# Two strips in one output tile, some stores issued by ScalarE, and a new order of work, in an attention and gated-convolution kernel

## The chip, the core and the metric

The kernel runs on one core of a Trainium2 chip. The metric is the device time of one execution in microseconds (us), as the median of several executions. The core's engines work side by side: TensorE does matmuls (PE; its weight loads are PEld), VectorE (DVE), ScalarE (ACT) and GpSimd (POOL) do elementwise work, and SyncE (SP) issues DMAs. ScalarE can issue DMAs as well; these are listed under ACTq, those of SyncE under SPq.

## What is computed

The reference is two stages of attention with 32 learned points, and a gated convolution behind it (B=4, N=12800, C=128, 32 inducing points, 5 taps):

```python
def mab(q, kv):
    s = scale * (q @ kv.transpose(0, 2, 1))
    a = np.exp(s - s.max(-1, keepdims=True))
    a /= a.sum(-1, keepdims=True) + 1e-09
    return a @ kv
h = mab(I, x)          # 32 rows per batch, a sum over all of x
y = mab(x, h)          # 12800 rows per batch, 32 weights each
...
for k in range(K):
    gate_pre += conv_w[k][None, None, :] * yp[:, k:k + S, :]
gate = 1.0 / (1.0 + np.exp(-gate_pre))
out = (gate * (y @ w_val)) @ w_out
```

Since y is 32 weights per row times h, the kernel never writes y: five taps and the value product are six small matrices of 32x128 per batch (W), which are applied to the 32 softmax weights of each row (P).

## The kernel before, in words

**Tiles.** A batch of 12800 rows is cut into four strips of 3200, which lie side by side: a strip takes 32 of the 128 partitions or columns of PE. The strips are cut into chunks of 128 to 512 columns (SIZES), 29 chunks in all over the four batches. An array `seqs` numbers them from 0 to 28; the last one, 28, has 160 columns, number 27 has 512.

**Stages of a batch**, each an item of the list ORDER (lines 957 to 998) by a short name:

- `l`, `k`: loads of x by SP, `xt` with channels on partitions (load_xt, L359) and `xk` with rows on partitions (load_xk, L370). For batch 0 nearly all of xk is made by transposes on PE instead (`x`, make_xk, L397) and evicted by ACT (L402) or DVE (L404), as XEV says.
- `s1` (L422): scores of a chunk against the 32 points, evicted by DVE with the maximum (L430). `gm` (gmax, L441 to 457): the maximum of a group of chunks (GROUPS), over the strips on POOL.
- `h` (L465 to 497): exponentials on ACT, a transpose on DVE, and the matmuls of xk that sum h (L486).
- `u`, `t`, `w`, `W`, `po`: preparation: h from the groups' sums (u, L528 to 536), its transpose (t, L545), the small matrices in two fp16 parts (w, L565 to 603; the last inputs are written in L587 and L603), their transposes onto the strips (W, L621, evicted in L629 and L631), and the scaled output weights (po).
- `s2` (L691 to 749): scores of a chunk against h, softmax over 32 on DVE, POOL and ACT, into P in two fp16 parts.
- `r` (rblock, L763 and L772): a row block. It runs gate and value matmuls of up to three neighbouring chunks on the four row groups of PE at the same time. Two row blocks belong to a chunk. `begun` (L188) splits the gate units (15 per strip) over neighbouring blocks; the constant EVEN weighs an even split. Behind it come tanh on ACT (L833), the product of gate and value on DVE (L843), and two fp16 parts of it (halves: L856 on ACT, L861 on POOL, tile `gl`).
- `o` (outp, L865): the output matmul of one strip of a chunk (three fp16 matmuls, L881 to L883; for chunk 28 one fp32 matmul, L874), its eviction with scaling by DVE or ACT (L891 or L893; DVE where 4 x chunk + strip stands in OUTV), and its store by SP (L898). The tiles are `os`, four buffers; in the last two chunks `et`, `pt` and `ss`, which are free by then.
- `z` (idle, L917): n matmuls on zeros, which compute nothing that is used.

**What sets the order.** PE follows ORDER as it stands. Everything else is ordered by a planner in the kernel itself (Plan.order and Plan.lay, L79 to L184): it lays the operations on their engines with the durations in COST, the DMA rate BW, and due times worked out backwards from PE's list, and takes at each moment the ready operation with the earliest due time, less the operation's entry in URGE. SP issues in the order that results. A load planned when AHEAD or more row blocks are already in the list waits for the row block that many back (`ago`, L332). BUFS gives the buffers of each tile: 11 for xt, 4 for xk, 4 for os, 4 PSUM banks `a`.

The output function before, cut to the choice of tiles and the store:

```python
        if k >= len(seqs) - 2:
            os = ("ss" if k == len(seqs) - 1 else ("et", "et", "et", "pt")[r], "out", b, c, r)
        ...
        def store():
            nc.sync.dma_start(out[b, :, r, FIRST[b][c]:FIRST[b][c] + n], st[os][:, :n])

        op("SP", n * 512 / BW, store, [j], 0.0, [], [os])
```

Of the kernel before, what the change touches and what calls it, by code (L numbers as in the profile page):

```python
# [20 lines left out]
P = 128  # L21
# [28 lines left out]
class Plan:  # L50
# [85 lines left out]
    def lay(self, deps, succ, topo, nominal):  # L136
# [18 lines left out]
        while len(seq) < n:  # L155
# [14 lines left out]
            if e == "SP":  # L170
                bus = max(bus, start) + ops[i]["dur"]
                end[i] = max(bus, start + 0.5) + (1.7 if start < 10.0 else 2.6)
                free[e] = start + 0.4
# [39 lines left out]
def tile_kernel(ctx: ExitStack, tc: tile.TileContext, xt, xk, indT_in, w64, out):  # L213
# [651 lines left out]
    def outp(k, r):  # L865
# [4 lines left out]
        if k >= len(seqs) - 2:  # L870
            os = ("ss" if k == len(seqs) - 1 else ("et", "et", "et", "pt")[r], "out", b, c, r)
        if k == len(seqs) - 1:
# [14 lines left out]

        def ev():
            o, a = sb(pw, os, [P, 512])[:, :n], st[key][:, :n]
            if v:  # L890
                V.tensor_scalar(o, a, st["osc", b], None, ALU.mult)  # L891
            else:
                S.activation(o, a, AF.Copy, scale=st["osc", b])  # L893

        j = op("DVE" if v else "ACT", cost("psum", n) + 0.07 if v else cost("act", n) + 0.06, ev, [i], 0.0, [os], [key, ("osc", b)])

        def store():
            nc.sync.dma_start(out[b, :, r, FIRST[b][c]:FIRST[b][c] + n], st[os][:, :n])  # L898

        op("SP", n * 512 / BW, store, [j], 0.0, [], [os])  # L900


# [53 lines left out]
GROUPS = [[[0, 1], [2, 3, 4], [5, 6, 7]], [[0, 1, 2, 3], [4, 5, 6]], [[0, 1, 2], [3, 4, 5, 6]], [[0, 1, 2], [3, 4, 5, 6]]]  # L956
ORDER = [
# [40 lines left out]
]  # L998
XEV = ["SSSV", "SVSS", "SVSS", "SSSV", "SSSS", "SSVS", "SVSS", "SSVS"]
URGE = {  # L1000
    "e1.f": -13,
    "s2.sub": 8,
    "s2.hi": -28,
    "s2.lo": 7.5,
    "s2.tout": -6.5,
    "s2.ex": 1.5,
    "s2.tin": -3.5,
    "rblock.gv": -5,
    "s2.sm": -2.5,
    "make_xk.ev": 1.5,  # L1010
    "h.acc": -4,
# [72 lines left out]
```

## Time and profile before

| what | value |
|---|---|
| median of 3 runs | 288.19 us (287.75 to 290.25) |
| profiled execution, its own time | 288.69 us |
| its span | 286.6 us |
| granted TensorE clock, mean | 0.996 |
| PE busy | 278.0 us |
| DVE, ACT, POOL busy | 230.4, 204.6, 214.2 us |
| matmuls on zeros in items z (L917) | 31 |
| HBM read, written | 47.63 MB, 26.21 MB |

All other numbers are those of the profiled execution. A row of the order of time or of the chain begins with the start in us from the span's start and the length in us. "<-" between tiles means "written from"; "<-" in brackets names what ended an engine's wait. The chain of waits is followed back from the end: what released each step, or what stood before it on its engine. A PE that is busy on zeros counts as busy.

### The profile page before, as it was taken

The numbers are of one execution on the slowest core, as the hardware profiler recorded it, in microseconds if no ns is written. First come the engines' busy times: TensorE is split into PE (matmuls) and PEld (weight loads), VectorE is DVE, ScalarE is ACT, GpSimd is POOL, SyncE is SP. The second block draws the span as 40 slices with busy tenths as digits, with TensorE's granted clock in tenths as the row PEclk, the third lists the DMA queues.
The fourth block names the chain that finished last, engine by engine and source line by source line (L and its number), as shares of the span: only waits on it lengthen the run. The fifth ranks groups of instructions, "written<-read, shape, count | busy, mean of one in ns | idle before, by whom it ended". The sixth has DMA issues, their size and how long they took to land.

```text
span 286.6 us, 10022 instructions
## 1 busy us (share of the span) xinstructions
PE 278.0 (97%) x4038; PEld 136.0 (47%) x4038; DVE 230.4 (80%) x574; ACT 204.6 (71%) x310; POOL 214.2 (75%) x256
## 2 busy tenths in 40 slices
PE   8899999999999999999999999999999999999992
PEld 3467546464335335555454645644334443433450
DVE  1458899999999999769789899897896986844551
ACT  2363344578785769767787579897799787888792
POOL 1122077887899989959498989998899999865770
PEclk9999999999999999999999999999999999999998
DMA  7999999999987979998647993234233343443545
GB/s 250 408 418 421 415 387 365 414 392 395 361 314 234 403 274 294 413 363 267 239 160 234 342 387 109 106 125 159 88 132 130 129 148 128 156 146 148 189 159 194
DMA packets 24382, 74.50 MB, mean 260 GB/s; under 512 B 2832, under 2 KB 12560, under 8 KB 22160
## 3 DMA queue, kind: packets, MB, share of 16 engines
q1 hardware_dynamic: 24192, 73.84, 69.0%
q8 instruction: 32, 0.52, 0.7%
q14 instruction: 14, 0.11, 0.1%
q10 hardware_dynamic: 144, 0.02, 0.0%
HBM read 47.63 MB, written 26.21 MB: 258 GB/s over the span
## 4 chain that ended last, share of the span: by engine, by line
PE 90%; DVE 4%; DMA 3%; issue 0%; SPq 0%; ACT 0%
PE g L763 29%; PE a L881 10%; PE a L486 8%; PE a L691 8%; PE a L883 7%; PE a L882 7%; PE a L772 7%; PE a L422 7%; PE g L397 3%; DMA xt<-in_xt_dram 3%; PE g L917 2%; PE a L621 1%; DVE ss L430 1%; DVE e L697 1%; PE a L528 1%; PE a L874 0%
## 5 line engine op out<-in xcount | busy, mean ns | idle before, releaser
L861 POOL TENSOR_TENSOR gl<-tg,gh 128x1024 f16<-128x1024 f32 (+4 forms) x56 | 106.5, 1906 | 18.0 <-ACT gh L856 15.7
L763 PE MATMUL g<-P,W 32*128 32x448 f16 (+5 forms) x1740 | 109.7, 345 | 0.0
L833 ACT ACTIVATE tg<-g,gsc 128x1024 f32<-128x1024 f32 (+5 forms) x58 | 57.8, 996 | 29.4 <-PE g L763 24.9
L843 DVE SCALAR_TENSOR_TENSOR tg<-tg,a 128x512 f32<-128x512 f32 (+5 forms) x116 | 65.5, 602 | 11.7 <-PE a L772 10.8
L763 PEld LDWEIGHTS <-W 32*128 32x128 f16 x1740 | 50.6, 92 | 43.2 <-issue 13.1
L856 ACT CAST gh<-tg 128x1024 f16<-128x1024 f32 (+4 forms) x56 | 52.7, 946 | 0.6 <-PE a L882 0.2
L772 PE MATMUL a<-P,W 32*128 32x512 f16 (+5 forms) x348 | 42.7, 348 | 0.0
L893 ACT ACTIVATE os<-a,osc 128x512 f32<-128x512 f32 (+4 forms) x63 | 38.1, 633 | 5.5 <-PE a L883 5.3
L881 PE MATMUL a<-gh,wo 128*128 128x512 f16 (+4 forms) x112 | 40.2, 359 | 0.0
L882 PE MATMUL a<-gh,wo 128*128 128x512 f16 (+4 forms) x112 | 39.6, 354 | 0.0
L883 PE MATMUL a<-gl,wo 128*128 128x512 f16 (+4 forms) x112 | 39.6, 354 | 0.0
L891 DVE TENSOR_SCALAR os<-a,osc 128x448 f32<-128x448 f32 (+4 forms) x45 | 29.6, 674 | 7.8 <-PE a L883 7.4
L749 POOL TENSOR_TENSOR P<-pt,P 128x512 f16<-128x512 f32 (+4 forms) x29 | 29.9, 1038 | 2.6 <-ACT P L742 2.4
L731 POOL TENSOR_TENSOR e<-e,z 128x512 f32<-128x512 f32 (+4 forms) x29 | 27.1, 938 | 4.9 <-DVE z L723 2.5
L708 POOL TENSOR_TENSOR e<-e,m 128x512 f32<-128x512 f32 (+4 forms) x29 | 27.1, 938 | 3.1 <-DVE m L702 3.0
L422 PE MATMUL a<-xt,indT 128*32 128x512 f32 (+5 forms) x232 | 27.3, 540 | 1.3 <-DVE ss L430 0.9
L486 PE MATMUL a<-xk,et 128*32 128x129 f32 x800 | 28.1, 275 | 0.4 <-issue 0.3
L486 PEld LDWEIGHTS a<-xk,et 128*32 128x32 f32 x800 | 23.3, 109 | 8.2 <-issue 3.7
L691 PE MATMUL a<-xt,hT 128*32 128x512 f32 (+4 forms) x232 | 27.0, 544 | 0.0
L430 DVE TENSOR_SCALAR_CACHE_REDUCE ss<-a 128x512 f32<-128x512 f32 (+5 forms) x29 | 17.4, 603 | 11.9 <-PE a L422 11.6
L714 ACT ACTIVATE e<-e 128x512 f32<-128x512 f32 (+4 forms) x29 | 16.5, 576 | 10.5 <-POOL e L708 10.4
L881 PEld LDWEIGHTS <-wo 128*128 128x128 f16 x112 | 10.9, 97 | 27.4 <-issue 18.2
(107 smaller groups left out, 326.0 us busy)
## 6 DMA issues: line engine op xcount, KB each, us to landing
xt<-in_xt_dram SPq DMA_DIRECT2D x11, 1024.0 KB, 7.8
out_dram<-os SPq DMA_DIRECT2D x36, 256.0 KB, 3.8
xk<-in_xk_dram SPq DMA_DIRECT2D x10, 903.0 KB, 7.9
out_dram<-os SPq DMA_DIRECT2D x40, 224.0 KB, 2.4
xt<-in_xt_dram SPq DMA_DIRECT2D x8, 896.0 KB, 9.4
xk<-in_xk_dram SPq DMA_DIRECT2D x6, 1032.0 KB, 8.5
xt<-in_xt_dram SPq DMA_DIRECT2D x6, 960.0 KB, 8.0
xk<-in_xk_dram SPq DMA_DIRECT2D x5, 967.5 KB, 9.7
```

Source lines behind the costliest of these rows:

```text
L422: T.matmul(s[32 * r:32 * r + 32, :n], c_["indT"], x[:, o:o + n // 32, r, :], start=True, stop=True)
L486: T.matmul(t[32 * s:32 * s + 32, :P + 1], e[:, 32 * i:32 * i + 32], x[:, m + i, :], start=i < R, stop=i >= nb - R)
L691: T.matmul(s[32 * r:32 * r + 32, :n], st["hT", b], x[:, m:m + nb, r, :], start=True, stop=True)
L763: T.matmul(st[f"g{r // 2}", b, c][:, r % 2, :n], st["W", b][q, w, k, :], st[("P1", "P2")[e]][q, o:o + n], start=u == 0, stop=u == len(taps ...
L772: T.matmul(st["a", "v", b, c, r][:, :n], st["W", b][q, w, TAPS, :], st[("P1", "P2")[e]][q, o:o + n], start=u == 0, stop=u == 2)
L833: S.activation(t[:, :, :n], st[f"g{p}", b, c][:, :, :n], AF.Tanh, scale=st["gsc", b])
L843: V.scalar_tensor_tensor(t, t, 1.0, st["a", "v", b, c, r][:, :n], ALU.add, ALU.mult)
L856: S.copy(sb(pw, g1, [P, 2, 512], F16)[:, :, :n], st[tg][:, :, :n])
L861: G.tensor_tensor(sb(pw, g2, [P, 2, 512], F16)[:, :, :n], st[tg][:, :, :n], st[g1][:, :, :n], ALU.subtract)
L881: T.matmul(t, w[:, 0], st[g1][:, q, :n], start=True, stop=False)
L882: T.matmul(t, w[:, 1], st[g1][:, q, :n], start=False, stop=False)
L883: T.matmul(t, w[:, 0], st[g2][:, q, :n], start=False, stop=True)
```

## The change

Four edits in `outp` and one group of constants.

1. **Last chunk (28).** Its four strips go in pairs into two `ss` tiles of 512 columns (strip q of the pair at q x 160), and each pair is stored by one DMA of SP, which waits for both evictions. Before, there were four tiles and four stores.
2. **Last chunk but one (27).** Strips that ACT evicts are also stored from ACT's own queue; strips that DVE evicts are stored by SP as before. By the new OUTV strips 0 and 3 are ACT's, 1 and 2 are DVE's; before, 3 alone was DVE's.
3. The planner counts 0.45 us for an SP issue instead of 0.4 and may place the stores on ACT.
4. **Constants.** ORDER, GROUPS of batch 0, XEV, URGE, EVEN, OUTV (98 entries to 103) and AHEAD (19 to 25) are others. In ORDER the items z have 21 matmuls instead of 31. Chunk 2 of batch 0 is now loaded second (0, 2, 1, 4, 3, then the weights); the first group of batch 0 has chunks 0, 1 and 2 instead of 0 and 1. In the preparation of batch 0 the two W items stand ahead of 13 matmuls on zeros, where one of them stood behind 18. BUFS is the same.

```diff
-                free[e] = start + 0.4
+                free[e] = start + 0.45
...
+        last = k == len(seqs) - 1
+        if last:
+            os = ("ss", "out", b, c, p)
+        elif k == len(seqs) - 2:
+            os = (("et", "et", "et", "pt")[r], "out", b, c, r)
...
+        new = not last or q == 0
+
         def ev():
-            o, a = sb(pw, os, [P, 512])[:, :n], st[key][:, :n]
+            if new:
+                sb(pw, os, [P, 512])
+            at = q * n if last else 0
+            o, a = st[os][:, at:at + n], st[key][:, :n]
...
+        if last:
+            if q:
+                def store():
+                    nc.sync.dma_start(out[b, :, r - 1:r + 1, FIRST[b][c]:FIRST[b][c] + n],
+                                      st[os][:, :2 * n].rearrange("p (r t) -> p r t", r=2))
+
+                op("SP", 2 * n * 512 / BW, store, [ix["out", k, r - 1], j], 0.0, [], [os])
+        elif k == len(seqs) - 2 and not v:
+            def store():
+                S.dma_start(out[b, :, r, FIRST[b][c]:FIRST[b][c] + n], st[os][:, :n])
+
+            j = op("ACT", 0.45, store, [j], 0.0, [], [os], lag=2.3)
+            op("NOP", 0.0, lambda: None, [j])
+        else:
+            def store():
+                nc.sync.dma_start(out[b, :, r, FIRST[b][c]:FIRST[b][c] + n], st[os][:, :n])
+
+            op("SP", n * 512 / BW, store, [j], 0.0, [], [os])
...
-GROUPS = [[[0, 1], [2, 3, 4], [5, 6, 7]], ...
+GROUPS = [[[0, 1, 2], [3, 4], [5, 6, 7]], ...
 ORDER = [
-    ("z", 0, 3), ("l", 0, 0), ("s1", 0, 0), ("x", 0, 0), ("s1", 0, 1), ("z", 1, 6), ("gm", 0, 0), ("x", 0, 1),
-    ("s1", 0, 2), ("l", 0, 4), ("l", 0, 3), ("l", 0, 7), ("z", 4, 1), ("l", 0, 1), ("l", 0, 6), ("x", 0, 2),
...
-    ("h", 0, 7), ("s1", 1, 1), ("u", 0), ("z", 5, 3), ("gm", 1, 0), ("l", 1, 0), ("l", 1, 1), ("t", 0), ("w", 0),
-    ("s2", 0, 0), ("s2", 0, 1), ("s2", 0, 2), ("z", 2, 18), ("W", 0, 0), ("s2", 0, 3), ("s2", 0, 4), ("W", 0, 1),
-    ("h", 1, 0), ("s2", 0, 5), ("l", 1, 2), ("r", -1, 1), ("r", 0, 0), ("h", 1, 3), ("s1", 1, 4), ("h", 1, 2),
...
-    ("o", 26, 0), ("r", 28, 0), ("o", 26, 2), ("o", 26, 3), ("r", 28, 1), ("r", 29, 0), ("o", 27, 0), ("o", 28, 1),
-    ("o", 28, 2), ("o", 28, 0), ("o", 28, 3), ("o", 27, 1), ("o", 27, 3), ("o", 27, 2),
+    ("z", 1, 4), ("l", 0, 0), ("l", 0, 2), ("z", 4, 1), ("l", 0, 1), ("l", 0, 4), ("l", 0, 3), ("raw",), ("l", 0, 6),
+    ("x", 0, 0), ("k", 0, 4), ("s1", 0, 0), ("z", 0, 1), ("l", 0, 7), ("l", 0, 5), ("s1", 0, 2), ("s1", 0, 1),
+    ("gm", 0, 0), ("x", 0, 2), ("x", 0, 1), ("h", 0, 0), ("s1", 0, 4), ("s1", 0, 3), ("h", 0, 2), ("gm", 0, 1),
...
+    ("s1", 1, 1), ("u", 0), ("z", 5, 2), ("t", 0), ("w", 0), ("l", 1, 0), ("s2", 0, 1), ("s1", 1, 3), ("s2", 0, 0),
+    ("gm", 1, 0), ("W", 0, 0), ("s2", 0, 2), ("W", 0, 1), ("z", 2, 13), ("s2", 0, 3), ("s2", 0, 4), ("h", 1, 0),
+    ("h", 1, 1), ("r", -1, 1), ("po", 0), ("h", 1, 2), ("r", 0, 0), ("s1", 1, 4), ("h", 1, 3), ("s1", 1, 5),
...
+    ("o", 26, 0), ("r", 28, 0), ("o", 26, 2), ("o", 26, 3), ("r", 28, 1), ("r", 29, 0), ("o", 28, 0), ("o", 27, 1),
+    ("o", 27, 0), ("o", 28, 2), ("o", 28, 3), ("o", 27, 2), ("o", 27, 3), ("o", 28, 1),
 ]
-XEV = ["SSSV", "SVSS", "SVSS", "SSSV", "SSSS", "SSVS", "SVSS", "SSVS"]
+XEV = ["SVVV", "SSSV", "SVSV", "SSSS", "SSSS", "SSVS", "SSSS", "SSSS"]
...
-EVEN = 0.04765998428116873
+EVEN = 0.0469045735303122
...
-AHEAD = 19
+AHEAD = 25
```

More of the change, by code (lines that the diff above doesn't have):

```diff
@@ L869, in outp @@
         key, os = ("a", "o", b, c, r), ("os", b, c, r)
-        if k >= len(seqs) - 2:
-            os = ("ss" if k == len(seqs) - 1 else ("et", "et", "et", "pt")[r], "out", b, c, r)
-        if k == len(seqs) - 1:
+        last = k == len(seqs) - 1
[4 more added lines that the diff above has]
+        if last:
             def f():
@@ L893, in ev @@
                 S.activation(o, a, AF.Copy, scale=st["osc", b])
[L895 to L900, printed above, removed]
+        j = ix["out", k, r] = op("DVE" if v else "ACT", cost("psum", n) + 0.07 if v else cost("act", n) + 0.06, ev, [i], 0.0,
+                                 [os] * new, [key, ("osc", b)] + [os] * (not new))
+        if last:
+            if q:
[12 more added lines that the diff above has]
+            op("SP", n * 512 / BW, store, [j], 0.0, [], [os])
     def warm_up():
@@ L953, in tile_kernel @@
     return plan
-GROUPS = [[[0, 1], [2, 3, 4], [5, 6, 7]], [[0, 1, 2, 3], [4, 5, 6]], [[0, 1, 2], [3, 4, 5, 6]], [[0, 1, 2], [3, 4, 5, 6]]]
+GROUPS = [[[0, 1, 2], [3, 4], [5, 6, 7]], [[0, 1, 2, 3], [4, 5, 6]], [[0, 1, 2], [3, 4, 5, 6]], [[0, 1, 2], [3, 4, 5, 6]]]
 ORDER = [
[40 rows of a table removed]
[40 rows of a table added]
 ]
-XEV = ["SSSV", "SVSS", "SVSS", "SSSV", "SSSS", "SSVS", "SVSS", "SSVS"]
+XEV = ["SVVV", "SSSV", "SVSV", "SSSS", "SSSS", "SSVS", "SSSS", "SSSS"]
 URGE = {
[L1001 to L1007, printed above, removed]
-    "rblock.gv": -5,
-    "s2.sm": -2.5,
-    "make_xk.ev": 1.5,
-    "h.acc": -4,
-    "halves.lo": -1,
-    "s2.mx": 5.5,
-    "s1.g": -5.5,
-    "s2.nm": -3,
-    "halves.hi": -2,
-    "e1.tr": -4.5,
-    "evac.ev": -20.5,
-    "rblock.th": 8,
-    "values.gv": -4,
-    "rows.th": -8,
-    "gmax.f1": 4,
-    "gmax.f0": 1,
-    "outp.ev": 4,
+    "e1.f": -3,
+    "s2.sub": 14,
+    "s2.hi": -37.5,
+    "s2.lo": -0.5,
+    "s2.tout": -6,
+    "s2.ex": 3,
+    "s2.tin": 0.5,
+    "rblock.gv": -5,
+    "s2.sm": -2,
+    "make_xk.ev": 14,
+    "h.acc": -2,
+    "halves.lo": -0.5,
+    "s2.mx": 4.5,
+    "s1.g": -6.5,
+    "s2.nm": 9.5,
+    "halves.hi": -3,
+    "e1.tr": -2.5,
+    "evac.ev": -18.5,
+    "rblock.th": 9,
+    "values.gv": 5,
+    "rows.th": -6.5,
+    "gmax.f1": 28,
+    "gmax.f0": 1.5,
+    "outp.ev": 18,
 }
 TURNED = (0,)
-EVEN = 0.04765998428116873
+EVEN = 0.0469045735303122
 OUTV = [
[4 rows of a table removed]
[5 rows of a table added]
 ]
```

74 rows, old and new, of tables (ORDER, OUTV) are left out of this document.

## The prediction

> **What bounds the kernel now.** I read the page first: busy shares and the chain that ended last.
>
> ```profile
> span 286.6 us, 10022 instructions
> PE 278.0 (97%) x4038; PEld 136.0 (47%) x4038; DVE 230.4 (80%) x574; ACT 204.6 (71%) x310; POOL 214.2 (75%) x256
> ...
> PE 90%; DVE 4%; DMA 3%; issue 0%; SPq 0%; ACT 0%
> ```
>
> PE carries 90% of the chain; the rest is DVE and DMA. A table by stage shows where PE is not full (columns: length, then busy time of PE, PEld, DVE, ACT, POOL, granted clock, DMA share, GB/s).
>
> ```profile
> 10.00:20.00 10.00, 9.05 (x102) 5.51 (x95) 5.67 (x16) 5.25 (x9) 1.49 (x7) 1.00 1.01 424
> ...
> 43.00:53.00 10.00, 9.83 (x243) 6.04 (x236) 9.69 (x28) 5.33 (x11) 8.06 (x16) 1.00 0.97 375
> ...
> 60.00:80.00 20.00, 20.00 (x299) 9.49 (x302) 19.13 (x51) 15.39 (x27) 16.50 (x20) 1.00 1.01 377
> 80.00:100.00 20.00, 20.00 (x274) 8.42 (x270) 19.36 (x47) 14.32 (x20) 19.04 (x17) 1.00 0.86 312
> ...
> 240.00:260.00 20.00, 20.00 (x248) 7.88 (x244) 13.17 (x22) 15.87 (x20) 16.12 (x10) 1.00 0.40 144
> ```
>
> From 60 on PE is full in every stage, and DVE is all but full with it until 100. In this part time can go only if PE is given less to do. The front, up to the first row block, is different: PE is busy there too, but partly with matmuls on zeros (item z, L917), which compute nothing. So it may be gained or lost there. The third place is the tail, after PE's last matmul.
>
> **The change part by part.**
>
> *Tail.* The order of time near the end (start, length, what; SPq and ACTq are the queues' issues):
>
> ```profile
> 278.05 1.32 PE a L874 x8
> ...
> 281.35 0.69 ACT et L893
> ...
> L893 ACT ACTIVATE ss<-a,osc x3: 387/393/395, 278.7 to 279.4; 128x160 f32<-128x160 f32 x3
> ...
> 279.23 2.81 SPq L898 DMA_DIRECT2D out_dram<-ss  x4
> 282.13 0.38 SPq L898 DMA_DIRECT2D out_dram<-et  x1
> ...
> 283.08 0.41 SPq L898 DMA_DIRECT2D out_dram<-et  x1
> ...
> SPq L1079 <- DMA out_dram<-et: 2.0, 1, 2.0
> ...
> 0.71 0.41 ACTq L254 DMA_DIRECT2D indT<-in_indT_dram  x1
> ...
> 283.00:284.00 1.00, 0.00 (x0) 0.00 (x0) 0.00 (x0) 0.00 (x0) 0.00 (x0) 1.00 1.01 391
> 284.00:285.00 1.00, 0.00 (x0) 0.00 (x0) 0.00 (x0) 0.00 (x0) 0.00 (x0) 0.68 1.01 389
> ```
>
> PE's last matmul ends at X = 281.35, the last eviction at 282.04, yet the last store is issued only at 283.08, or X+1.73: four small stores held SP's queue to 282.04, and three stores of 256 KB follow, the third issued 0.95 after the first, 0.48 a step. The landing is 2.0 us behind the end of the last issue (283.49), at 285.5. The DMA engines are full from 283 to 285.
>
> After the change the last units are 27.2 (DVE, SP), 27.3 (ACT, ACT's queue) and 28.1 (ACT, SP; one store for two strips). 27.3 leaves PE one small unit (1.32/4 of L874) before X, that is at X-0.33; its eviction ends at X+0.36, that of 28.1 (0.39, the median of the small ones now) at X+0.75. Then both queues issue at once, SP for the pair, ACT for 27.3: X+0.8 instead of X+1.73. Behind that lie 256+160 KB instead of the three stores' 768 KB. With the same way from issue to landing as now (0.41+2.0) the end comes 0.9 earlier; with the shorter transfer 352 KB less at 390 GB/s would be another 0.9, half of it hidden because 27.2 still drains before. I take 1.1. Bounds: 0.2 (ACT issues 27.3's store, 0.41, ahead of 28.1's eviction, and the pair's issue is as long as the longest of the small ones, 1.34 in the row below) to 1.4 (transfer shorter and no queue). The two store issues on ACT, 0.41 each, lie beside PE, in the room that 27.1's eviction (0.69) leaves as it goes to DVE. Queued behind the first issue is 28.3's small eviction, which its store has to wait for some 0.4 longer, 1 us before X and so still ahead of the last two.
>
> ```profile
> L898 SPq DMA_DIRECT2D out_dram<-ss x4: 383/403/1343, 279.2 to 280.7; - x4
> ...
> 274.97 4.39 POOL L861 TENSOR_TENSOR gl<-tg,gh 128x1024 f16<-128x1024 f32 x2 [1.75 <-ACT gh L856]
> ...
> 280.02 0.22 PE a L881
> ```
>
> A new wait is possible on PE: strips 2 and 3 of chunk 27 need POOL's last gl, ready at 279.36. Now they start at 280.02 (0.66 spare); in the new order 28.1 comes behind them and they start 0.33 earlier. So the cover is 0.33: I cost it at nothing, 0.3 if POOL is that much later.
>
> The Trainium skill, "DMA: Bandwidth & Descriptors", section "Issuing engines are not separate DMA queues", speaks against the second queue: all issues run on the same 16 engines and interleave, so that a second issuer saves only issue time. By that rule the tail gains two steps of 0.48, 0.96 instead of 1.1, and the sum would be 0.1 smaller. The rows at 283 to 285 (engines full) agree with it.
>
> *Switches and row units on PE.* The first matmul after a change between row blocks, full-array and strip matmuls costs more:
>
> ```profile
> 272.11 0.32 PE a L881
> 272.44 0.22 PE a L882
> ```
>
> That is 0.10 a switch. Counted in ORDER by kind there are 163 switches before and 155 after; of the 8 fewer, 4 lie in the row blocks (142 to 138): 0.4. EVEN moves one entry of the unit split (8,1 becomes 9,0), 256 columns less on the longest strip, at 0.22/512 each 0.1. Together 0.5; bounds 0.1 (other costs hide in the switch) to 0.9.
>
> *The front.* The fillers go from 31 to 21, in the loads from 3+6+1 to 4+1+1 and in the preparation of batch 0 from 3+18 to 2+13.
>
> ```profile
> 1.63 7.74 DMA xt<-in_xt_dram
> ...
> 9.41 1.06 PE a L422 x8
> ...
> 14.49 1.06 PE a L422 x8
> ...
> 1.17 3.51 PE L906 MATMUL a<-zero 128*128 128x512 f16 x8 [1.17 <-DVE warm L240]
> ...
> 6.77 1.47 PE L917 MATMUL g<-zero 128*128 128x512 f16 x6
> ...
> 12.48 1.06 PE L422 MATMUL a<-xt,indT 128*32 128x512 f32 x8
> ...
> 36.28 1.70 PE a L691 x24
> 37.98 3.99 PE g L917 x18
> ...
> 39.07 0.25 DVE L603 SCALAR_TENSOR_TENSOR w<-a,vs,w 128x32 f16<-128x32 f32 x1
> ...
> 41.97 0.45 PE a L621 x24
> ...
> 12.59 1.23 DVE L404 COPY xk<-g 128x1024 f32<-128x1024 f32 x1 [0.79 <-PE g L397]
> ```
>
> A filler is 3.99/18 = 0.22, so 10 are 2.2 us. In the loads I take the gain as nearly nothing: chunk 2 (third, 9.41) is now loaded before chunk 1, so it lands about 512 KB/424 GB/s = 1.2 earlier, at 8.2; PE is through with chunks 0 and 1 at 6.77 now (the row of 6 fillers), and with chunk 0 and two more fillers at about 6.8 then; it waits 1.4 where it now runs zeros. On the other side the gap from 13.54 to 14.49 gets h work of group 0 to fill it: -0.3 net. In the preparation the W transposes start only at 41.9, behind the 18 fillers, though their last input is written at 39.32 (L603). After: from 36.28 s2 of chunks 1 and 0 and one s1 of batch 1 come before W, 864 columns where the 1.70 are for 928, so 1.6; PE is there at 37.9, waits 1.4 for L603, does W, s2, W, and then 13 fillers (2.9). So 3.99 of zeros become 1.4 wait + 2.9 zeros: +0.3. What it wins is that W is ready 2.6 earlier. The 4 switches saved here give -0.4. Front together: -0.4. Bounds: -2.6 (all fillers and switches were pure cost) to +1.0 (the load order makes PE wait a further landing step of 1.2, with 0.2 of it covered).
>
> ```profile
> L891 DVE TENSOR_SCALAR os<-a,osc 128x448 f32<-128x448 f32 (+4 forms) x45 | 29.6, 674 | 7.8 <-PE a L883 7.4
> ```
>
> One eviction of xk (1.23) goes from DVE to ACT, 5 output evictions net go to DVE (98 to 103 in OUTV). Two of them fall to chunks 5 to 9, near 80 to 100, where DVE has 0.64 left for 2 x 0.67: 0 to +0.7; I take 0, as four PSUM buffers stand between. The others fall where DVE has 6.8 of 20 free. GROUPS, URGE and AHEAD only move work beside PE; at nothing, with the price under the last rival.
>
> **Sum.** -1.1 - 0.5 - 0.4 = -2.0. The profiled execution took 288.69 (span 286.6 and 2.1 around it); the median of the three runs is 288.19. From its own time the sum gives 286.7, from the median 286.2; I forecast between, **286.4**, 0.6% below the median. All times below count from this middle, 288.4. A measurement of this kernel can tell about 1% from no change: 285.3 and 291.1 are the limits.
>
> **The rivals.**
>
> A, *the fillers were pure cost.* The W row speaks for it (2.6 late behind zeros), the full DVE from 43 to 53 against it: whatever PE gains there, DVE takes back. -1.1 - 0.5 - 2.6: 284.2.
>
> B, *the front gives back.* DMA is at 424 GB/s from 10 on, and PE follows the landings; a first group of three chunks needs more landed before its maximum. Front +1.0 instead of -0.4: 287.8. For it: DMA 1.01 full. Against: the gap at 13.54.
>
> A variant of B: with fewer zeros a wait of PE grows to 3 us and the clock falls. In the tail rows the clock is 1.00 until 284 and 0.68 on average from 284 to 285, so it falls some 3.0 after the last matmul; the first eight matmuls of the run (3.51/8, 0.44 apart) show what the slow state costs: 8 x (0.44-0.22), 1.7 us. My longest wait is 1.4, so I give it little, inside B. The Trainium skill, "TensorE: Matmul & The Clock Gate", section "Part 1: The HAM clock gate (the "warmup" mystery)", has the window as about 3.4 us; the row's 3.0 is near it.
>
> C, *slower: SP's queue stops behind a load.* AHEAD 25 lets loads stand earlier in SP's order, and SP works in order: stores behind a load that waits for an xk buffer leave late, the four os buffers stay taken, evictions wait, and PE for their banks.
>
> ```profile
> SPq L370 <- PE a L486: 9.3, 5, 4.0
> ...
> 54.90 0.81 PE g L763 x26
> ...
> DMA to landing us min/median/max: 3.7/5.1/8.2
> ```
>
> Between 54 and 140 SP waits five times for xk, 9.3 in all; stores from 54 to 80 land after up to 8.2, and PE still had no idle time. From 54.9 on (the first long row block) a chunk takes (281.3-54.9)/29 = 7.8, so a store beyond about 8.2 holds its buffer into the next chunk: that is the point from which it decides. Five more such waits, half of them passed on: +4.7 - 2.0, 291.1. Against: AHEAD bars only loads planned with that many row blocks already in the list, the last six chunks of batch 3 now and the last three then; the others keep their place but for the new order.
>
> **How the numbers follow.** The forecast's own case, 285.3 to 287.5, 0.50; A 0.22; B 0.17; C 0.11. The range 283.9 to 289.1 leaves out the lower 0.4 of A (0.09) and nearly all of C (0.10). Faster by over 1%: nearly all of A (0.20) and a tenth of the forecast's case (0.05): 0.25. Slower by over 1%: half of C and a little of the unknown, 0.08. Within 1%: 0.67.
>
> **What would show it.** Right: PE's last matmul about 0.9 earlier in the span, the last store issue under 1 us behind it and not 1.73, the last 2 us of DMA no longer full; L917 with 21 matmuls, and wait rows of PE before 10 and 40 of about 1.4 each; PE still 20 of 20 from 60 to 260. Wrong: PE under 19.8 of 20 in a stage after 60 (C); PE waits at 35 to 45 under 0.5 in all (A); the first gate matmul later than now, with DVE under 9 of 10 around it (B); an ACT store issue far above 0.41, or a last landing over 3 us behind its issue, would break the tail's step.

## The result, and the profile after

| | before | after |
|---|---|---|
| median of 7 runs each | 288.83 us (287.75 to 290.25) | 286.12 us (285.99 to 287.72) |
| profiled execution, its own time | 288.69 us | 286.11 us |
| its span | 286.6 us | 284.3 us |

The ratio is 0.991, with a 95% interval of 0.988 to 0.994: 2.5 us less, where 2.0 were forecast, and the median lies 0.3 below the forecast time. The size was right. Of the terms behind it, the tail's was too large and had another cause than the one given, that for switches and row units did not come, and the front's was too small. That they add up to about the right time is luck.

The page after; its line numbers moved: the output matmuls are L884 to L886 and L877 (fp32), the evictions L899 (DVE) and L901 (ACT), the stores L908 (pairs), L914 (ACT's queue) and L920 (SP), the matmuls on zeros L939.

```profile
PE 276.2 (97%) x4028; PEld 136.5 (48%) x4028; DVE 232.2 (82%) x577; ACT 203.2 (71%) x307; POOL 214.0 (75%) x256
...
PE 94%; DVE 2%; issue 1%; ACT 1%; POOL 0%; POOLq 0%
```

PE is busy for 1.8 us less and has ten matmuls fewer; the 3% of DMA are gone from the chain. The stages after, with the columns of the table before:

```profile
60.00:80.00 20.00, 20.00 (x309) 9.25 (x302) 19.16 (x51) 14.74 (x25) 18.02 (x21) 1.00 0.98 360
...
280.00:281.00 1.00, 0.00 (x0) 0.00 (x0) 0.00 (x0) 0.09 (x1) 0.00 (x0) 1.00 1.02 371
281.00:282.00 1.00, 0.00 (x0) 0.00 (x0) 0.00 (x0) 0.00 (x0) 0.00 (x0) 1.00 0.97 332
282.00:283.00 1.00, 0.00 (x0) 0.00 (x0) 0.00 (x0) 0.00 (x0) 0.00 (x0) 1.00 0.08 25
```

From 60 to 80 PE and DVE are as full as before, and at the end the DMA engines are full to 282. PE's last wait ahead of W after (us in total, times, longest):

```profile
PE a L565 <- DVE hT L548: 0.3, 1, 0.3
```

It waits there for 0.3; the two waits of 1.4, in the loads and ahead of W, that were forecast are in no row (from 8 to 13, in the loads, PE sits idle for 0.8 in all). The order of time after shows why, first the loads (s1 of chunks 2 and 1), then what lies between L565 and the transposes of W (L621):

```profile
7.21 1.50 PE L422 MATMUL a<-xt,indT 128*32 128x512 f32 x16
...
34.27 0.41 PE L565 MATMUL a<-hT,w 128*128 128x32 f32 x2 [0.28 <-DVE hT L548]
...
35.31 0.45 DVE L697 STREAM_TRANSPOSE e<-a 128x256 f32<-128x256 f32 x1
...
35.84 0.41 DVE L702 TENSOR_REDUCE m<-e 128x8 f32<-128x256 f32 x1
...
36.27 0.52 PE L621 MATMUL a<-ident,w 128*32 128x128 f16 x24
...
36.44 0.25 DVE L603 SCALAR_TENSOR_TENSOR w<-a,vs,w 128x32 f16<-128x32 f32 x1
```

The same stretch before, where L565 started at 35.87 and L603 at 39.07; DVE's rows alone:

```profile
36.88 0.33 DVE L697 STREAM_TRANSPOSE e<-a 128x160 f32<-128x160 f32 x1
37.13 0.11 DVE L609 TENSOR_SCALAR gsc<-gmx 128x1 f32<-128x1 f32 x1
37.16 0.20 DVE L610 TENSOR_SCALAR q<-wrow,vmx 128x1 f32<-128x1 f32 x1
37.28 0.31 DVE L702 TENSOR_REDUCE m<-e 128x5 f32<-128x160 f32 x1
37.51 0.44 DVE L697 STREAM_TRANSPOSE e<-a 128x256 f32<-128x256 f32 x1
37.93 0.65 DVE L470 STREAM_TRANSPOSE et<-ss 128x448 f32<-128x448 f32 x1
38.50 0.38 DVE L702 TENSOR_REDUCE m<-e 128x8 f32<-128x256 f32 x1
```

DVE put 2.1 us of s2 and h work (L697, L702, L470) into this stretch before and 0.9 after. So L603 starts 2.2 behind L565 and not 3.2, and the transposes of W start at 36.27 and not at 41.9. In the loads, s1 of chunk 2 is under way from 7.2 on; the forecast had the chunk landing at 8.2. The end of the order of time:

```profile
278.92 0.44 PE L877 MATMUL a<-tg,wof 128*128 128x160 f32 x2
...
279.84 0.34 ACTq L914 DMA_DIRECT2D out_dram<-pt  x1
280.12 0.38 SPq L908 DMA_DIRECT2D out_dram<-ss  x1
```

PE ends at 279.36, and the last store is issued 0.76 behind it (1.73 by the forecast's reading of before, 1.77 from PE's end at 281.31). Taken by itself, this looks as the forecast said. But that store takes 3.3 us to land, where the last one before took 2.5.

### The profile page after: what moved, and what is told of

Its sections match the earlier page's. It is cut to its first block, busy times and chain, and to the rows that moved or that the text cites. A ratio compares the mean times of both kernels' runs of the same rounds, so it can differ in the third digit from the quotient of the medians.

```text
span 284.3 us, 9991 instructions
## 1 busy us (share of the span) xinstructions
PE 276.2 (97%) x4028; PEld 136.5 (48%) x4028; DVE 232.2 (82%) x577; ACT 203.2 (71%) x307; POOL 214.0 (75%) x256
## 4 chain that ended last, share of the span: by engine, by line
PE 94%; DVE 2%; issue 1%; ACT 1%; POOL 0%; POOLq 0%
PE g L763 30%; PE a L884 9%; PE a L486 9%; PE a L691 8%; PE a L422 8%; PE a L772 8%; PE a L886 7%; PE a L885 7%; PE g L397 2%; PE g L939 2%; PE a L928 1%; PE a L621 1%; DVE ss L430 1%; PE a L528 1%; DVE os L899 0%
## 5 line engine op out<-in xcount | busy, mean ns | idle before, releaser
L901 ACT ACTIVATE os<-a,osc 128x448 f32<-128x448 f32 (+4 forms) x60 | 36.5, 632 | 6.2 <-PE a L886 5.7
L884 PE MATMUL a<-gh,wo 128*128 128x512 f16 (+4 forms) x112 | 40.1, 359 | 0.0
L886 PE MATMUL a<-gl,wo 128*128 128x512 f16 (+4 forms) x112 | 39.6, 354 | 0.0
L899 DVE TENSOR_SCALAR os<-a,osc 128x448 f32<-128x448 f32 (+4 forms) x48 | 31.4, 670 | 9.6 <-PE a L886 9.4
L422 PE MATMUL a<-xt,indT 128*32 128x512 f32 (+5 forms) x232 | 27.3, 538 | 0.0
L884 PEld LDWEIGHTS <-wo 128*128 128x128 f16 x112 | 10.9, 97 | 25.0 <-issue 18.2
```

What stands on the lines that cost most here:

```text
L422: T.matmul(s[32 * r:32 * r + 32, :n], c_["indT"], x[:, o:o + n // 32, r, :], start=True, stop=True)
L884: T.matmul(t, w[:, 0], st[g1][:, q, :n], start=True, stop=False)
L886: T.matmul(t, w[:, 0], st[g2][:, q, :n], start=False, stop=True)
```

## The experiments

The theory at first was the forecast's: the tail gains 1.1 because SP's queue was held by four small stores, and the fillers (the matmuls on zeros) cover work of DVE and loads, so that their number means little. The rivals: A, the fillers were pure cost; C, stores leave late. Each run is compared with the kernel before on the same chip; differences in us are the ratio times its median there, 288.4 to 288.6.

**1. The kernel before with 21 fillers.** Only three numbers in ORDER change; the planner, which counts fillers, moved a few operations of other engines with them.

```diff
-("z", 1, 6) ... ("z", 5, 3) ... ("z", 2, 18)
+("z", 1, 2) ... ("z", 5, 2) ... ("z", 2, 13)
```

> The kernel before with 21 instead of 31 matmuls on zeros (items z 3, 2, 1, 2, 13 where it has 3, 6, 1, 3, 18) and nothing else changed. Theory F, the ten fillers were pure cost in the old order too: span 286.6 - 2.2 = 284.4, about the changed kernel's 284.3. Theory O, the gain comes from the new order of loads and preparation, and in the old order the fillers only cover waits (chunk 2 lands at 9.41, W's input is written at 39.32, 2.6 us ahead of its use): of the four in the loads nothing is won, the six in the preparation shorten a stretch that is late by 2.6, so at most -1.3: span 285.3 to 286.6. PE then shows the missing time as waits.

Measured: 286.78 us, ratio 0.9955 (0.9938 to 0.9973), 1.3 us less. That is the edge of what the forecast's theory allowed (0 to 1.3), and not the full 2.2 of ten fillers. But in its trace PE's last matmul ends at 280.59, only 0.7 ahead of before, and the last store is issued 0.79 behind it, with the old tail. That was the first sign against the tail's term.

**2. The changed kernel without the 13 fillers behind W.**

```diff
-("W", 0, 1), ("z", 2, 13), ("s2", 0, 3)
+("W", 0, 1), ("s2", 0, 3)
```

> The changed kernel without its 13 fillers between the second W item and s2 of chunk 3; 8 fillers are left. Theory F: another 13 x 0.22 = 2.9 less, span 281.4. Theory C, cover: DVE, which is 98% busy from 40 to 50, sets the pace there, PE waits instead, span 284.3 within 0.4. If a wait of PE grows to about 3 us the granted clock falls and the span goes up by up to 1.7.

Measured: 286.67 us, ratio 0.9949 (0.9931 to 0.9967), no faster than the changed kernel. The stage where the 13 stood, and PE's longest wait of this kernel:

```profile
40.00:50.00 10.00, 7.53 (x206) 5.45 (x206) 9.75 (x29) 4.55 (x10) 6.76 (x14) 1.00 1.02 415
```

```profile
PE a L486 <- DVE et L470: 2.4, 3, 1.7
```

PE lost 2.5 of the 10 us to waits, beside a DVE that is 9.75 busy; the 13 fillers were about 2.9. These are cover: DVE sets the pace there. For them rival A is wrong.

**3. The kernel before with the new tail alone** (the edits in `outp`, the last eight items of ORDER and the entries of OUTV for the last two chunks; the other engines' order is that of before up to the tail).

```diff
-("o", 27, 0), ("o", 28, 1), ("o", 28, 2), ("o", 28, 0), ("o", 28, 3), ("o", 27, 1), ("o", 27, 3), ("o", 27, 2)
+("o", 28, 0), ("o", 27, 1), ("o", 27, 0), ("o", 28, 2), ("o", 28, 3), ("o", 27, 2), ("o", 27, 3), ("o", 28, 1)
```

> The kernel before with the changed tail alone: pairs of strips of the last chunk in one tile and store, ACT's queue for its stores of the last chunk but one, the new order of the last eight output items and their new engines (DVE for 27.1, 27.2 and 28.2). My prediction's step: 1.1 less, span 285.5. Theory D, the tail is bound by the data of the last stores and not by their issue: span 286.6 within 0.3, the last issue about 1.0 behind the last matmul and DMA full for the last 3.5 us of data.

Measured: 287.25 us, ratio 0.9960 (0.9940 to 0.9981), 1.15 us less. That is the 1.1 of the forecast. It seemed to prove the tail's term, until the sixth run. In its profile PE also ends at 280.14, 0.6 to 1.2 ahead of the three executions of before, and most of that lead is there before the tail begins.

**4. A large unit last**: in the changed kernel ("o", 28, 1) stands before ("o", 27, 2).

```diff
-("o", 28, 3), ("o", 27, 2), ("o", 27, 3), ("o", 28, 1),
+("o", 28, 3), ("o", 28, 1), ("o", 27, 2), ("o", 27, 3),
```

> The changed kernel with strip 1 of the last chunk ahead of strips 2 and 3 of chunk 27, so that the store of two short strips (rows of 640 bytes) isn't the last. If the bytes of all last stores set the end: span 284.3 within 0.3, since the bytes are the same. If the short rows trickle at the end (after 282.0 the DMA engines of the changed kernel move 33 and 17 GB/s for 1 us): span 283.3 to 283.8, with no trickle behind the full stretch. By the issue times alone it would be the same or 0.3 later, as the last eviction is now one of 512 columns.

Measured: 286.82 us, ratio 0.9948 (0.9929 to 0.9968): not told apart from the changed kernel. The landing after the last issue does not decide, then. A row of the order of time and the stage around it show something else, an output eviction on DVE that stood idle for 2.08 us before it started:

```profile
101.87 0.75 DVE L899 TENSOR_SCALAR os<-a,osc 128x512 f32<-128x512 f32 x1 [2.08 <-PE a L422]
```

```profile
100.00:200.00 100.00, 99.30 (x1570) 51.46 (x1570) 87.22 (x223) 78.61 (x124) 88.07 (x105) 1.00 0.69 251
```

PE loses 0.7 us in this stage. If what the eviction waits for is one of the four os buffers, this is rival C in small; the eighth run tries that.

**5. and 6. The changed kernel again, and the changed kernel with the old tail** (the code of `outp`, the last eight items and the OUTV entries of before; the reverse of the third run).

> The changed kernel itself once more, beside the three below on the same chip: 0.991 of before, executions near 286.1, with some near 287.4.

> The changed kernel with the old tail: four tiles and four stores for the last chunk, all stores by SP, the old order of the last eight output items, and the old engines for the last eight strips (DVE for 27.3 and 28.0). By my prediction's step the new tail is worth 1.1, so 1.1 slower than the changed kernel, about 287.2. If the old tail costs extra only in those executions in which a small store's issue takes 1.34 instead of 0.39, the two are the same within 0.3, or the old one is better. Theory D (data of the last stores alone) also says the same within 0.3.

Measured: 286.76 us, ratio 0.9927 (0.9901 to 0.9953), for the first; 286.24 us, ratio 0.9909 (0.9881 to 0.9938), for the old tail. Without the new tail nothing is lost. The row of the four small stores in the old-tail kernel (min, median and max in ns), then PE's last matmuls and the last issue in its order of time:

```profile
L898 SPq DMA_DIRECT2D out_dram<-ss x4: 381/392/407, 277.6 to 279.1; - x4
```

```profile
279.31 0.38 PE L883 MATMUL a<-gl,wo 128*128 128x512 f16 x1
...
280.48 0.41 SPq L898 DMA_DIRECT2D out_dram<-et  x1
```

Four small stores do not hold the queue: 0.39 each, and the last of three large ones goes out 0.79 behind PE's end at 279.69. The row of before had the same median, 403, and a maximum of 1343. One issue was long, not four in a row. What lengthened it was the new question.

**7. The changed kernel with 31 fillers, counted by the planner** (7, 1, 2, 3 and 18 in place of 4, 1, 1, 2 and 13).

> The changed kernel with 31 fillers as before (items z 7, 1, 2, 3, 18 where it has 4, 1, 1, 2, 13). Theory F, each filler costs its 0.22: 2.2 slower, 288.3, span 286.5. Theory C, a filler costs only where PE would not wait anyway: the three more at the start come ahead of the first landing (PE waits for x there) and the one at 2 lies in the chain of the preparation, both free; the five after the second W item cost what is not covered by DVE, up to 1.1: 286.1 to 287.3.

Measured: 290.46 us, ratio 1.0061 (1.0039 to 1.0083), 3.7 more than the changed kernel. It isn't clean: with other counts the planner put DVE, ACT, POOL and SP into another order. The tenth run repeats it without that.

**8. The changed kernel with a fifth os buffer.**

```diff
-bufs=BUFS[key[0]], padded_shape=pad)
+bufs=BUFS[key[0]] + (key[0] == "os"), padded_shape=pad)
```

> The changed kernel with five os buffers instead of four, the order on every engine the same. In two of the runs so far DVE sat idle for 2.08 ahead of an output eviction at 101.9 though PE had written the strip by 100.1, and PE then lost 0.8. If that wait is for a store that still holds the os buffer, a fifth buffer removes it: all executions near 286.1, none near 287.4, and median 0 to 0.5 below the changed kernel's. If it is another wait, the two groups of times stay.

Measured: 285.82 us, ratio 0.9902 (0.9868 to 0.9935), the lowest median of all, though the interval does not tell it from the changed kernel's. The stage, the eviction of the fourth run, and a wait of PE:

```profile
100.00:200.00 100.00, 100.00 (x1575) 51.50 (x1574) 88.53 (x227) 79.59 (x125) 89.22 (x106) 1.00 0.69 250
```

```profile
100.86 0.75 DVE L899 TENSOR_SCALAR os<-a,osc 128x512 f32<-128x512 f32 x1 [0.31 <-PE a L886]
```

```profile
PE a L422 <- DMA xt<-in_xt_dram: 0.7, 1, 0.7
```

With one buffer more the eviction waits 0.31, and PE loses nothing from 100 to 200. But the changed kernel's two profiles (after and run 5) lose nothing there either: PE is busy for 100.00 of 100 in both, though the eviction waits 1.22 and 0.66. In run 8 0.7 was lost instead to a load that landed late, and PE ends at 279.84, later than in after (279.36). What makes this execution faster than after lies behind PE's end: 5.96 instead of 6.75. The part on the tail says what that is.

**9. The kernel before, issuing ten fillers fewer while the planner still counts 31**, so that every other engine keeps its order.

```diff
-            for _ in range(n):
+            for _ in range(n + {0: 0, 1: -4, 4: 0, 5: -1, 2: -5}[k]):
```

> The kernel before with ten fillers fewer (2 instead of 6, 2 instead of 3, 13 instead of 18), where the planner still reckons with 31, so that every other engine keeps its order of before. If the ten were pure cost (rival A): PE's last matmul 2.2 earlier than in an execution of before with the same landings, and about 286.2 in time. If each only filled a wait (my step for the loads): 0 to 0.5 of it, about 288. The earlier run with 21 fillers, in which the planner reordered a little, had PE's end 0.7 earlier than the one profile of before.

Measured: 286.89 us, ratio 0.9948 (0.9936 to 0.9961), 1.5 us less. Four views of this kernel: the queue q8 of the page, which carries instructions (packets, MB, share); the small stores; the stretch up to PE's end; the last issue.

```profile
q8 instruction: 31, 0.51, 0.7%
```

```profile
L898 SPq DMA_DIRECT2D out_dram<-ss x4: 382/388/402, 278.3 to 279.8; - x4
```

```profile
0.00:280.38 280.38, 276.53 (x4028) 135.36 (x4028) 230.34 (x574) 204.09 (x309) 214.11 (x256) 1.00 0.70 262
```

```profile
281.19 0.41 SPq L898 DMA_DIRECT2D out_dram<-et  x1
```

PE's end is 280.38. The three profiled executions of before (two of them are runs 11 and 12) have 281.31, 280.74 and 281.03, so ten fillers bring 0.4 to 0.9 there; the rest of their time turned into waits. Behind PE's end the same edit, which touches nothing near the tail, brings 0.8 to 1.7: the long small store is gone, and the last issue is 0.81 behind PE. And q8 has 31 packets, where the page of before has 32:

```profile
q8 instruction: 32, 0.52, 0.7%
```

**10. The changed kernel, issuing ten fillers more while the planner still counts 21.**

```diff
-            for _ in range(n):
+            for _ in range(n + {1: 3, 4: 0, 0: 1, 5: 1, 2: 5}[k]):
```

> The changed kernel with ten fillers more at its own places (three ahead of the first transposes, one after them, one in the preparation, five after the second W item), the planner reckoning with 21, so that every other engine keeps the changed kernel's order. Rival A, pure cost: 2.2 slower than the changed kernel, 288.3 to 288.9. Cover: the first four wait for the first landings anyway and the one lies in a chain, so at most the five, 0 to 1.1 slower: 286.2 to 287.5. The earlier run with 31 was 3.7 slower, but there the planner had set DVE, ACT, POOL and SP in another order; this run says how much of the 3.7 was that order.

Measured: 288.83 us, ratio 1.0018 (1.0002 to 1.0034); the median is 2.1 to 2.7 above the changed kernel's two. Its stretch up to PE's end, and its early and late fillers:

```profile
0.00:282.88 282.88, 279.64 (x4038) 137.26 (x4038) 233.48 (x577) 202.60 (x306) 213.96 (x256) 1.00 0.70 260
```

```profile
4.56 3.28 PE L939 MATMUL g<-zero 128*128 128x512 f16 x8
...
39.96 4.06 PE L939 MATMUL g<-zero 128*128 128x512 f16 x18
```

PE is busy for 3.2 us more than in the changed kernel's two executions (276.2 and 276.6) and ends 3.2 later (282.88 against the mean of 279.36 and 280.07): in the new order ten more fillers cost their full time. It is more than 10 x 0.22 because early matmuls are dearer (the last section); against run 5 alone, which was slow for as long at the start, PE is busy for 3.0 more and ends 2.8 later. Rival A is right for fillers added to this order and wrong for the old one. q8 has 32 packets here again, and one pair's issue takes 0.80 instead of 0.39.

**11. and 12. The kernel before, two more looks**, to see whether the long store belongs to the kernel or to one execution.

> The kernel before once more, for a second profile. If its tail always has one small store that takes 1.34 to issue, the last store is issued 1.7 behind the last matmul again and the time is 7.3 behind PE's end; if that was one execution's accident, 0.8 behind and 6.3. PE's end: 281.3 again, or up to 1.2 earlier if the landings of the first loads vary from one execution to the next, as the run with the new tail on the old front suggests (280.1).

> The kernel before a third time, as the run above: the same two questions.

Measured: 288.85 and 288.21 us. Both have it. The issue in the order of time and the instruction packet in the view of DMA queues, cut to the microsecond that holds it (280 to 281 in before, 279 to 280 in run 11; packets, MB, share), first of before, then of run 11; of run 12 the issue alone, as its packet's row is like that of run 11:

```profile
280.70 1.34 SPq L898 DMA_DIRECT2D out_dram<-ss  x1
```

```profile
q8 instruction: 1, 0.02, 5.8%
```

```profile
279.62 1.89 SPq L898 DMA_DIRECT2D out_dram<-ss  x1
```

```profile
q8 instruction: 1, 0.02, 11.1%
```

```profile
279.91 1.14 SPq L898 DMA_DIRECT2D out_dram<-ss  x1
```

Each time one packet of 16 KB and one long issue meet in the tail: in 3 of 3 executions of before. In runs 1, 6 and 9, with ten fillers fewer and the old tail, no such packet lies between 276 and 284, and no small store took over 0.41. It isn't only the tail. Counted over SP's issues behind 5 us in the three traces of before, 22 of the 65 that overlap a q8 packet took over 0.7 us, and 7 of the 413 that don't; in the profiled execution after it is 7 of 22 and 6 of 133.

## Why the prediction was right or wrong

**By parts.** The stretch up to the end of PE's last matmul, in the profiled executions of before and after:

```profile
0.00:281.31 281.31, 277.96 (x4038) 136.04 (x4038) 230.27 (x574) 203.94 (x309) 214.15 (x256) 1.00 0.70 262
```

```profile
0.00:279.36 279.36, 276.21 (x4028) 136.50 (x4028) 232.22 (x577) 202.45 (x306) 214.01 (x256) 1.00 0.70 263
```

The same stretches, counting the matmuls on zeros alone (all of them, the eight of the warm-up included):

```profile
0.00:281.31 281.31, 10.89 (x39) 3.88 (x39) 0.27 (x1) 1.00 0.70 262
```

```profile
0.00:279.36 279.36, 8.92 (x29) 3.02 (x29) 0.27 (x1) 1.00 0.70 263
```

The same for all executions that matter (us); "behind" is the execution's own time less PE's end:

| | PE's end | PE busy | of it on zeros | PE idle | behind |
|---|---|---|---|---|---|
| before (and runs 11, 12) | 281.31, 280.74, 281.03 | 277.96, 278.10, 278.81 | 10.89, 11.21, 11.61 | 3.35, 2.64, 2.22 | 7.38, 8.11, 7.18 |
| after (and run 5) | 279.36, 280.07 | 276.21, 276.64 | 8.92, 9.76 | 3.15, 3.43 | 6.75, 6.76 |
| after with the old tail (6) | 279.69 | 276.04 | 8.57 | 3.65 | 6.34 |
| before, ten fillers fewer (9) | 280.38 | 276.53 | 9.46 | 3.85 | 6.41 |

By the means PE ends 1.3 earlier after than before (281.03 to 279.72), 1.9 by less work, all of it zeros, and -0.55 by more waiting, and 0.8 less lies behind it (7.56 to 6.75): 2.1 in all. Of the 0.8, 0.3 lies outside the span: the own time less the span is 2.1 in before and in runs 1, 9, 11 and 12, and 1.8 after and in runs 5 and 6. The number of fillers alone does not bring it (runs 1 and 9), and the old tail does not take it away (run 6); what it is stays open.

**The tail, -1.1: too large, and the wrong cause.** The last store lands 4.5 behind PE's end before (mean of three) and 4.1 after: 0.4 less. The failing step is "four small stores held SP's queue to 282.04". The row from which it was read says 383/403/1343: one issue was long. Leaving out ten matmuls on zeros 240 us earlier takes that away (run 9), and with them gone the old tail is no slower than the new one (runs 5 and 6). The packets of q8 keep pace with PE's list: in before and in runs 11 and 12 the last three start when PE has begun about 7590, 7860 and 8130 of its matmuls and weight loads. The lists with ten fillers fewer end at 8116 to 8119, and the packet that is missing there is the last, which fell into the tail. So in the old list the number of fillers decides over packet and long issue together. It is no rule by count alone: the list of run 7 ends at 8137, and its trace has no such packet. That the packet delays the issue is the likely reading of 22 of 65 against 7 of 413, and of the three long issues of the tail, which end 0.2 to 0.4 behind the packet's end; but no run changed the fetch alone.

Run 3, which gave just the 1.1 forecast, changes PE's last instructions too, and its packet comes at 286.0, behind the last landing. So it took the packet out of the tail as well (in its profile 3.0 us instead of 2.1 lie outside the span, and the packet falls there), and does not show what the stores are worth by themselves.

The Trainium skill, "Runtime: NRT & Kernel Launch", section "Instruction fetch mechanics", says that instructions are fetched in blocks of 16 KB through DMA queues and that crossing a block is mostly hidden. The 32 packets of q8, 0.52 MB in all, agree with the size (those of a second instruction queue, q14, are of 8 KB); whether PE itself ever waits for one, no row here shows. The cost that the section doesn't speak of is that of the others: the long issues were SP's.

What was said of the new stores did come true: issues of 0.33 to 0.39 on both queues, the last one 0.76 behind PE. But the old tail without the packet has 0.79, and the transfer ends late: the DMA engines are full until 282 in the new tail, so that "the last 2 us of DMA no longer full" holds for one of them. The landing of strip 27.3, in after and then in run 8, which issues the same stores (KB each, median us to landing), each with the q14 packet of that trace, in 281 to 282 and in 285 to 286:

```profile
out_dram<-pt ACTq DMA_DIRECT2D x1, 256.0 KB, 3.1
```

```profile
q14 instruction: 1, 0.01, 1.9%
```

```profile
out_dram<-pt ACTq DMA_DIRECT2D x1, 256.0 KB, 2.2
```

```profile
q14 instruction: 1, 0.01, 2.4%
```

The 3.1 is over the 3 us that the prediction named as a sign against the step. In after an instruction packet falls among the last stores, in run 8 it comes behind the last landing (282.99). The same in all traces (us; the landing is that of the last store, counted from PE's end):

| tail | executions | instruction packet among the last stores | last landing |
|---|---|---|---|
| old | before, runs 11, 12 | q8 | 4.3, 5.0, 4.1 |
| old | runs 1, 6, 9 | none | 3.3, 3.3, 3.3 |
| new | after, runs 2, 4, 5 | q14 | 4.1, 4.1, 3.9, 4.1 |
| new | run 10 | q8 and q14 | 4.3 |
| new | runs 3, 7, 8 | none | 3.2, 3.1, 3.1 |

Without a packet the new tail is worth 0.1 to 0.2; with one, either tail is late by 0.8 or more. So the change lost one packet from its tail (q8) and got another (q14). Late landing and packet go together in all 14 traces; that the packet causes it is the likely reading, and was not tried alone.

What the Trainium skill, "DMA: Bandwidth & Descriptors", section "Issuing engines are not separate DMA queues", says of a second issuer, that it saves only issue time, agrees with the rows without a packet: the last issue goes out 0.76 or 0.77 behind PE with two queues and 0.79 to 0.81 with one, so there is next to no issue time to save.

**Switches and row units, -0.5: not seen.** A gain of 0.5 would have to show in PE's busy time without the zeros: 267.07, 266.89 and 267.20 before, 267.29 and 266.88 after (run 9, with the old list: 267.07). The means are equal to 0.1, and executions of one kernel differ by up to 0.4. So the term is nothing, or well under what was forecast. The weak step is to count switches over the whole list by the price of one pair of rows (0.32 and 0.22). Another count was wrong without harm: only the entries of OUTV under 116 (29 chunks of four strips) name a strip, and these go from 47 to 51, so four evictions net went to DVE, not five.

**The front, -0.4: too small.** With no gain from the switches, all of the 1.3 at PE's end is the front's. The step that failed is "3.99 of zeros become 1.4 wait + 2.9 zeros". It kept the time that W's last input came behind L565 at that of the old order; but DVE had other work in that stretch, and the new order holds less of it there (2.1 and 0.9, the rows above). With the loads it was the same: chunk 2 was there before 7.2 and not at 8.2. It is not rival A either. Taken from the old order, ten fillers were worth 0.4 to 0.9 at PE's end: 1.8 less work by the means, 1.1 more waiting. After, PE waits 0.55 more than before, half of that. So the fillers taken out were mostly cover in the old order. Where the cover was can be seen at the first gate matmul: it starts at 44.89 in run 9, 1.2 ahead of the mean of before, but from 45 to 60 PE then waits 0.77 (0.16 to 0.44 in the three of before, nothing after). That the new order takes away part of what the fillers covered is the likely reading. How much of that is the loads' and how much is W's was not tried apart. The 13 that are left are cover (run 2), and ten more are pure cost (run 10). The sign that the prediction laid down for A, PE waits at 35 to 45 under 0.5, was met all the same (0.0, and 0.1 in run 5). It could tell nothing: the three executions of before have 0.4 there, under 0.5 as well.

**Rivals B and C.** B's sign, a later first gate matmul, did not come: it starts at 44.59 after and 45.42 in run 5, against 45.93 to 46.14 before. C did not come as a whole, but its place was right. The eviction near 101 waits for something that a fifth os buffer shortens (2.08 in run 4, 1.22 in after, 0.66 in run 5, 0.31 with the fifth buffer), and in run 4 it costs PE 0.7. Whether the buffer makes the kernel faster is not shown: 285.82 against 286.12 and 286.76 lies within the intervals, and in the profile of run 8 the gain lies in the tail, where the q14 packet has moved.

**Still open**: how a fetch of instructions would lengthen another engine's DMA issue or delay a landing, and what the 0.3 us outside the span are.

## What to carry to other kernels

Read the maximum beside the median in a row of several issues before you explain a queue: one of 1.3 us is another mechanism than four of 0.4. What a matmul on zeros is worth, nothing or its full time, depends on what stands behind it: try it by issuing fewer and more with every other engine's order held fixed. Before you credit an edit near the end of a kernel, look in the view of DMA queues for an instruction packet among the last stores, before and after: here traces with one landed 0.8 us later or more, whatever the stores. A part that gives just the expected gain when it is tried alone can still owe it to something else; taking the same part out of the full change is the check.

## What was unexpected of the hardware

Leaving out ten matmuls (run 9) took 0.7 to 1.5 us from one store's issue near the end (1343, 1887 and 1136 ns, against 402), with the place where a 16 KB packet of instructions falls. In 14 traces, a late last landing and an instruction packet among the last stores always came together.

Early matmuls on zeros are dearer than later ones: in run 10 3.28/8 = 0.41 us each before 7.8, 4.06/18 = 0.23 each at 40. They start 0.43 apart at first and 0.22 apart later, and the moment of the change differs between executions of the same kernel. The same five fillers, in after and then in run 5:

```profile
4.55 1.61 PE L939 MATMUL g<-zero 128*128 128x512 f16 x5
```

```profile
4.56 2.45 PE L939 MATMUL g<-zero 128*128 128x512 f16 x5
```

So the same five fillers take 0.8 more in run 5, by chance at the start and not by the kernel, and PE ends 0.7 later there.
